# A list scheduler with new costs and due times, and a tail by tiles, in a kernel of sparse attention and mixture of experts

## Chip, cores and metric

The kernel runs on one core of one Trainium2 chip. The metric is the device time of one execution in microseconds (us); of the kernel before three runs were timed, 705.86 to 707.34, median 705.9. The core has a matrix engine (TensorE, PE in the rows; its weight loads stand apart as PEld), a vector engine (VectorE, DVE), a scalar engine (ScalarE, ACT), GpSimd (POOL) and SyncE (SP), which here only issues loads.

## What is computed

Attention over 8 batches, 8 heads, 576 positions and 64 dimensions, whose first four heads look at the last 32 positions and whose other four at every 32nd; then a mixture of 8 experts over the 4608 rows of 512 that result, one expert per row:

```python
scores = q @ k^T / 8
mask = (0 <= rel < 32) for heads 0..3, (rel >= 0) & (pos % 32 equal) for heads 4..7
attn = exp(scores - max) / (sum(exp(scores - max)) + 1e-9)
x = (attn @ v), rows of all heads side by side          # 4608 x 512
logits = x @ w_gate; e = argmax(logits); gate = softmax(logits)[e]
out[row] = gate * (relu(x[row] @ w1[e]) @ w2[e])        # w1 512x1024, w2 1024x512
```

## The kernel before, in words

**Attention.** Only the score blocks that the masks leave are computed. A batch gives five *banks*, each a PSUM tile of 128x512; there are 40 of them, numbered in the order of the batches. A bank's path is `score_ops` (L591 on): PE writes the mask with one matmul (L601, PSUM tag `s`, two buffers) and adds 16 to 32 small products, local ones of 32x64 (L608) or strided ones of 54x54 (L618); DVE takes the maximum (L643) and subtracts it (L648), ACT takes the exponential (L652), DVE sums (L657) and makes the reciprocals of the sums (L659, L660), GpSimd multiplies (L664), PE transposes (L670, tag `t`), and ACT copies that out (L327). Then `product_ops` multiplies with v (L696) into the tags `v` and `w`, one buffer each, and ACT copies the result to `xT`.

**Routing.** Two batches are a *group* (four groups of 1152 rows). Per group `logit_ops` computes the logits (L817, L827), `row_ops` transposes the rows (L874) and writes them with their gate to a table in DRAM, and `route_ops` ranks the rows of each expert (L913) and adds to the lists of row numbers (L960, L964).

**Experts.** A *window* takes up to 4 tiles of 128 rows of one expert: gather from the table (L339), transpose (L421) and split each value into a high and a low part; then in 8 steps the first matmul (L449 to L451, three products per block, tag `t`), relu and split (L456, L459), and the second matmul (L469 to L471) into one accumulator per tile; each finished tile is scaled (L355, L357) and scattered to the output (L347). Weights come in loads of 1 MB, four for a window or slot, and are split by ACT (L330) and DVE (L333, `wlo`). After the second group is routed, windows of two tiles of the experts 0, 2, 4 and 6 (*early windows*) may start while attention goes on; the others follow the last group. Eight *slots* of one tile take the rows over 512 of an expert (L1156 to L1217). A loop that the chip decides on (L1255) would take further slots; with these inputs it turns no times.

**What sets the order.** Every step is an `Op` with an engine, a cost, dependences, a due time (`pri`) and the buffers it takes and gives. `Plan.run` imitates the engines: it picks, for the engine that can start first, the operation with the earliest due time among those that can start within `LOOK`, and emits it. So costs and due times, made from constants as `PACE`, `LEAD` and `FILL0` at the file's head, set the order in which each engine's queue is written, and each engine works its queue in that order. `Plan.issue` (L170 on) holds what the planner believes of PE: half speed after a quiet stretch, a cost for changing the shape of the array, and a pause where the count of instructions passes a multiple of 256.

Of the kernel before, what the change touches and what calls it, by code (L numbers as in the profile page):

```python
# [18 lines left out]
N = B * S  # L19
# [16 lines left out]
RSLOT = 8  # L36
# [6 lines left out]
XTAGS = ("yy", "yy", "vw", "vw")  # L43
# [5 lines left out]
PACE = 5.69  # L49
PACE2 = 4  # L50
LAG = 5.0
LEAD = 48.87
ROWLAG = 2.0
FILL0 = 4.87
FILLW = 40.13
WLEAD = 20.91
WSPL = 3.63
SLOTP = 1987.69
BASEP = 2000.0
GLEAD = 38.84  # L60
TLEAD = 22.28
# [38 lines left out]
FORM_COST = 1.14  # L100
LOOK = 0.3


class Op:
    def __init__(self, eng, cost, fn, deps, pri, take, give, form, nbytes, rate, ins):
        self.eng, self.cost, self.fn, self.pri, self.take, self.give = eng, cost, fn, pri, take, give
        self.form, self.nbytes, self.rate, self.ins = form, nbytes, rate, ins
# [11 lines left out]
class Plan:  # L119


    def __init__(self, bufs):
# [12 lines left out]
        self.hold = True  # L135

# [3 lines left out]
    def add(self, eng, cost, fn, deps=(), pri=0.0, take=(), give=(), form=FULL, nbytes=0, rate=380e3, ins=1):  # L140
        op = Op(eng, cost, fn, deps, pri, list(take), list(give), form, nbytes, rate, ins)
        op.hold = self.hold
        if nbytes and eng != POOL:
            lane = Token("lane", 1)
            op.take.append(lane)
            op.give.append(lane)
# [23 lines left out]
    def issue(self, op, start):  # L170
# [3 lines left out]
        if e == PE:  # L174
# [8 lines left out]
            end = start + op.cost / self.speed(start)  # L183
            done = end + SETTLE[e]
            x = start
            while x < end:
                w = int(x // 3.4133)
                y = min(end, (w + 1) * 3.4133)
                if y <= x:
                    y = end  # L190
                self.busy[w] = self.busy.get(w, 0.0) + y - x
                x = y
        if op.nbytes:
            self.dma = max(end + 0.9, self.dma) + op.nbytes / op.rate
            done = self.dma + 0.9
        self.t[e] = end
# [10 lines left out]
    def run(self, held=False):  # L207
# [5 lines left out]
        for op in ops:  # L213
            for d in op.deps:
# [7 lines left out]
        while must:  # L222
# [26 lines left out]
            for s in op.succ:  # L249
                s.left -= 1  # L250
                if s.left == 0:
                    s.at = max(d.done for d in s.deps)
# [16 lines left out]
def moe_attn(ctx, tc, lqk, vl, sqk, vs, wg, wcat, blob, out):  # L269
# [14 lines left out]
                 "route": 1, "sl": 2, "xge": 4, "xe": 1, "ye": 2, "xgm": 9, "xtm": 2, "yp": 5, "sx": 2, "shr": 2, "shh": 2,  # L284
# [76 lines left out]
    def weights(source, deps, pri, pools, after_row=None):  # L361
# [11 lines left out]
        ld = add(SP, 0.45, load, deps, pri, take=[traw], nbytes=128 * CHW * 4)  # L373
        parts = []
        for h in range(2):
# [8 lines left out]
            def lo(sl=sl):  # L384
                split_lo(w["raw"][:, sl], w["hi"][:, sl], w["lo"][:, sl])

            a = add(ACT, 1.05, hi, [ld] + parts[-1:], pri + WLEAD - WSPL + 0.2 * h, take=[twhl] if h == 0 else (), give=[traw])
            d = add(DVE, 1.23, lo, [a], pri + WLEAD - WSPL + 0.2 * h, give=[traw])
# [3 lines left out]
    def window(e, nt, idc, odc, deps, pri, pace, gp, xp, yp_, names, pools, rows=N + 1, width=512, vtags="vw", ytags=YTAGS):  # L392
# [6 lines left out]
        for t in range(nt):  # L399
# [6 lines left out]
            gs.append(add(POOL, 1.0, g, deps, pri - GLEAD, take=[tk], nbytes=128 * XW * 4, rate=250e3))  # L406
# [3 lines left out]
        for dc in range(4):  # L410
# [18 lines left out]
            p = before = add(PE, 0.109 * nt, tr, gs + [before], pri - TLEAD + 2.5 * dc, take=[tv] + ([txx] if dc == 0 else []), ins=2 * nt)  # L429
# [4 lines left out]
        prev = []  # L434
        last = None
        for c in range(NCH):
            p0 = pri + 2 * c * pace
            w, parts, twhl = weights(lambda e=e, c=c: wcat[(e * NCH + c) * 128:(e * NCH + c + 1) * 128, :], (), p0 - WLEAD, pools)
            for fl in range(2):
# [22 lines left out]
                def mm2(w=w, fl=fl, j=j, b=b):  # L462
# [3 lines left out]
                    for t in range(nt):  # L466
                        ts = slice(t * 128, (t + 1) * 128)
# [904 lines left out]
```

## Time and profile before

| what | us |
|---|---|
| three runs, median (lowest to highest) | 705.9 (705.86 to 707.34) |
| the profiled execution, its own time | 708.59 |
| its span, first to last instruction | 706.8 |
| PE busy (share of the span) | 641.9 (91%) |
| DVE busy | 449.1 (64%) |
| ACT busy | 350.5 (50%) |
| GpSimd busy | 147.0 (21%) |
| mean granted clock of TensorE | 0.958 |

PE's busy time counts matmuls whose ends are modelled, so that a busy PE may still be slow: at half the clock, or with products that follow each other loosely. Idle time of an engine is put down to what ended it; "issue" is idle time that no wait in the profile explains. The span is cut below at three moments: the first expert matmul, the last entry in the lists of rows, and the last matmul.

### The profile page before, as it was taken

The page shows a single profiled execution, that of the slowest core. Times are in us where ns is not written, and L with a number is a line of the kernel's source. Part 1 is how long each engine was busy: PE and PEld are TensorE (multiplying, and loading weights), DVE is VectorE, ACT ScalarE, POOL GpSimd, SP SyncE. Part 2 cuts the span into 40 slices and gives each one's busy share as a digit, 9 for nine tenths or more (in the row PEclk, how much of TensorE's full clock was granted, in tenths as well). Part 3 has the DMA queues.
Part 4 walks back from the last instruction along what each step waited for, and adds up shares of the span by engine and source line. Part 5 has one row for each costly group of instructions (what it writes and reads, how often), then busy time and mean ns, then how long its engine had stood idle before and what let it go on. Part 6 is the DMA issues. An engine that isn't in the chain of part 4 may idle for free.

```text
span 706.8 us, 16724 instructions
## 1 busy us (share of the span) xinstructions
PE 641.9 (91%) x7013; PEld 541.2 (77%) x7020; DVE 449.1 (64%) x791; ACT 350.5 (50%) x601; POOL 147.0 (21%) x189
## 2 busy tenths in 40 slices
PE   5788878799999888999999899999699999999992
PEld 3666666688678677988888798788698888898881
DVE  4576867665786769995555577556467555687210
ACT  2454555456375654464444565545466545576110
POOL 1222321410322424011102303020500300241002
PEclk9698999899999999999999999999899999999996
DMA  9887666835574476576344668565745854692001
GB/s 348 347 317 274 233 220 219 285 118 197 196 260 157 148 263 247 200 274 247 127 184 161 245 233 307 186 255 196 279 161 181 287 189 175 206 348 108 30 1 61
DMA packets 31949, 149.65 MB, mean 212 GB/s; under 512 B 4861, under 2 KB 4861, under 8 KB 21632
## 3 DMA queue, kind: packets, MB, share of 16 engines
q1 hardware_dynamic: 19584, 118.24, 46.1%
q0 software_dynamic: 6432, 20.26, 8.0%
q10 hardware_dynamic: 5856, 10.07, 3.8%
q8 instruction: 56, 0.92, 0.5%
q14 instruction: 21, 0.17, 0.1%
HBM read 129.38 MB, written 20.22 MB: 212 GB/s over the span
## 4 chain that ended last, share of the span: by engine, by line
PE 48%; issue 32%; DVE 7%; POOL 5%; DMA 4%; ACT 2%; POOLq 0%; ACTq 0%; DVEq 0%
PE t L449 4%; PE t L450 3%; PE t L451 3%; PE v L696 3%; PE t L670 3%; PE s L618 3%; POOL out_dram L347 3%; PE s L608 3%; PE y L469 3%; PE y L471 3%; PE y L470 3%; POOL xg L339 2%; DVE wlo L333 2%; PE t L1187 1%; PE t L1188 1%
## 5 line engine op out<-in xcount | busy, mean ns | idle before, releaser
L333 DVE TENSOR_TENSOR wlo<-raw,whi 128x1024 fp32r<-128x1024 f32 x160 | 195.1, 1236 | 57.1 <-ACT whi L330 54.9
L330 ACT CAST whi<-raw 128x1024 fp32r<-128x1024 f32 x160 | 164.6, 1049 | 21.9 <-PE w L1217 10.9
L449 PE MATMUL t<-xh,whi 128*128 128x256 f32 (+1 forms) x384 | 127.2, 331 | 0.0
L451 PE MATMUL t<-xh,wlo 128*128 128x256 f32 (+1 forms) x384 | 122.8, 320 | 0.0
L450 PE MATMUL t<-xl,whi 128*128 128x256 f32 (+1 forms) x384 | 122.5, 319 | 0.2 <-issue 0.2
L456 ACT ACTIVATE hh<-t 128x256 fp32r<-128x256 f32 (+1 forms) x96 | 43.6, 455 | 119.6 <-PE t L451 109.6
L459 DVE SCALAR_TENSOR_TENSOR hl<-t,hh 128x256 fp32r<-128x256 f32 (+1 forms) x96 | 48.5, 508 | 76.8 <-ACT hh L456 75.7
L469 PE MATMUL y<-whi,hh 128*128 128x512 f32 x192 | 79.5, 414 | 2.2 <-ACT hh L456 2.2
L450 PEld LDWEIGHTS t<-xl,whi 128*128 128x128 f32 x384 | 73.2, 191 | 5.9
L451 PEld LDWEIGHTS t<-xh,wlo 128*128 128x128 f32 x384 | 73.1, 190 | 6.0 <-issue 0.3
L449 PEld LDWEIGHTS t<-xh,whi 128*128 128x128 f32 x384 | 73.0, 190 | 6.0
L471 PE MATMUL y<-whi,hl 128*128 128x512 f32 x192 | 76.2, 397 | 0.5 <-DVE hl L459 0.5
L470 PE MATMUL y<-wlo,hh 128*128 128x512 f32 x192 | 75.8, 395 | 0.0
L664 POOL TENSOR_TENSOR prob<-prob,ri 128x512 f32<-128x512 f32 x40 | 43.2, 1082 | 138.3 <-DVE ri L660 72.3
L347 POOL DMA_INDIRECT out_dram<-y,soids x8 | 9.4, 1174 | 208.2 <-DVE y L357 207.9
L643 DVE TENSOR_REDUCE nm<-s 128x8 f32<-128x512 f32 x40 | 27.3, 683 | 32.1 <-PE s L618 17.4
L471 PEld LDWEIGHTS y<-whi,hl 128*128 128x128 f32 x192 | 36.3, 189 | 9.8 <-DVE hl L459 1.5
L469 PEld LDWEIGHTS y<-whi,hh 128*128 128x128 f32 x192 | 36.3, 189 | 7.9 <-ACT hh L456 2.4
L347 POOL DMA_INDIRECT out_dram<-y,oids x24 | 29.9, 1245 | 55.4 <-DVE y L357 44.6
L470 PEld LDWEIGHTS y<-wlo,hh 128*128 128x128 f32 x192 | 36.4, 190 | 5.5
L652 ACT ACTIVATE prob<-prob 128x512 f32<-128x512 f32 x40 | 25.4, 634 | 27.2 <-DVE prob L648 25.7
L327 ACT COPY pT<-t 128x512 f32<-128x512 f32 x40 | 23.1, 590 | 30.7 <-PE t L670 28.9
(166 smaller groups left out, 1253.0 us busy)
## 6 DMA issues: line engine op xcount, KB each, us to landing
raw<-in_wcat_dram SPq DMA_DIRECT2D x80, 1024.0 KB, 5.2
xd<-xr ACTq DMA_DIRECT2D x36, 264.0 KB, 5.2
lqk_sb<-in_lqk_dram SPq DMA_DIRECT2D x16, 592.0 KB, 8.0
sqk_sb<-in_sqk_dram SPq DMA_DIRECT2D x16, 576.0 KB, 6.9
vt<-in_vl_dram SPq DMA_DIRECT2D x16, 576.0 KB, 7.4
vst<-in_vs_dram SPq DMA_DIRECT2D x8, 704.0 KB, 5.3
xg<-xd,ids POOLq DMA_INDIRECT x24
out_dram<-y,oids POOLq DMA_INDIRECT x24
```

The lines of the kernel that those rows point to most:

```text
L330: nc.scalar.copy(out=hi, in_=src)
L333: nc.vector.tensor_tensor(out=lo, in0=src, in1=hi.bitcast(F32), op=ALU.subtract)
L347: i = nc.gpsimd.indirect_dma_start(out=out, out_offset=bass.IndirectOffsetOnAxis(ap=idc, axis=0), in_=y, in_offset=None, bounds_check=N - ...
L449: nc.tensor.matmul(hb[:, 0:n], w["hi"][:, s], xh[:, dc, :], start=(dc == 0), stop=False)
L450: nc.tensor.matmul(hb[:, 0:n], w["hi"][:, s], xl[:, dc, :], start=False, stop=False)
L451: nc.tensor.matmul(hb[:, 0:n], w["lo"][:, s], xh[:, dc, :], start=False, stop=(dc == 3))
L456: nc.scalar.activation(out=b["hh"][:, 0:n], in_=b["hb"][:, 0:n], func=AF.Relu)
L459: nc.vector.scalar_tensor_tensor(out=b["hl"][:, 0:n], in0=b["hb"][:, 0:n], scalar=0.0, in1=b["hh"][:, 0:n].bitcast(F32), op0=ALU.max, op1= ...
L469: nc.tensor.matmul(yb, b["hh"][:, ts], w["hi"][:, s], start=(j == 0), stop=False)
L470: nc.tensor.matmul(yb, b["hh"][:, ts], w["lo"][:, s], start=False, stop=False)
L471: nc.tensor.matmul(yb, b["hl"][:, ts], w["hi"][:, s], start=False, stop=(j == 7))
L664: nc.gpsimd.tensor_tensor(out=pv, in0=pv, in1=st["ri"].unsqueeze(2).broadcast_to([128, 8, 64]), op=ALU.mult)
```

## The change

The planner gets other costs and rules. Its count of PE's instructions starts 63 earlier and takes the local banks at 32 products where it took 16; a new block of 256 may start 2.2 us after it was asked for, plus up to 2.6 us of what the load queue still has to do. Half speed holds from the start of the program, and within an operation. DVE operations that are marked `lock` and those of GpSimd wait for each other. Operations of one `row` name keep their order among themselves. All due-time constants are new.

In the kernel itself: the constants are loaded in two parts (320 of 622 columns first) and the masks made in two steps; the sums go to fixed tiles, and their reciprocals are made by an operation of its own (`inverse`) through three-dimensional views; rows of the first two groups are transposed into `v` and `w` instead of `y`; logits are copied out by ACT instead of DVE; slots gather into a pool of their own; windows of odd experts with an even one before them transpose through `v`, `s`, `s` instead of `v`; the last window does its last two steps of the second matmul tile by tile; and the loop stands in a condition.

```diff
-XTAGS = ("yy", "yy", "vw", "vw")
+XTAGS = ("vw",) * 4
-PACE = 5.69
-PACE2 = 4
-LAG = 5.0
-LEAD = 48.87
-ROWLAG = 2.0
-FILL0 = 4.87
+PACE = 4.44
+PACE2 = 4.84
+LAG = 7.05
+LEAD = 22.82
+ROWLAG = -3.33
+FILL0 = 29.38
...
-            self.half[w] = w > 4 and self.busy.get(w - 1, 0.0) < 0.55 * 3.4133
+            self.half[w] = self.busy.get(w - 1, 0.0) < 0.55 * 3.4133
...
+        if op.eng == DVE and op.lock:
+            r = max(r, self.port[POOL] - 0.13)
+        elif op.eng == POOL:
+            r = max(r, self.port[DVE] - 0.1)
...
-            b = self.count // 256
+            b = (self.count + 63) // 256
             self.count += op.ins
-            if self.count // 256 != b:
-                start = max(start, self.block.get(b - 1, 0.0) + 3.3)
+            while (self.count + 63) // 256 > b:
+                b += 1
+                if b > 1:
+                    asked = self.block.get(b - 1, 0.0)
+                    start = max(start, asked + 2.2 + min(max(self.dma - asked, 0.0), 2.6))
                 self.block[b] = start
...
+                if tail and j >= 6:
+                    steps.append((mm2, d, parts[1], th, twhl))
...
+        if tail:
+            for t in range(nt):
+                for k, (mm2, d, part, th, twhl) in enumerate(steps):
+                    last = add(PE, 3 * 0.229, lambda mm2=mm2, t=t: mm2([t]), [d, part, last], pri + 8.5 * pace + 0.1 * t,
+                               give=[th, twhl], ins=6)
+                ends[t] = last
...
         def c_load():
-            nc.scalar.dma_start(out=cst, in_=blob)
+            nc.scalar.dma_start(out=cst[:, 0:cm], in_=blob[:, 0:cm])
+
+        def c_rest():
+            nc.scalar.dma_start(out=cst[:, cm:], in_=blob[:, cm:])
...
-                sm = small.tile([128, 8], F32, name="sm")
-                nc.vector.tensor_reduce(out=sm, in_=pv, axis=AX.X, op=ALU.add)
-                st["ri"] = small.tile([128, 8], F32, name="ri")
-                nc.vector.tensor_scalar(out=st["ri"], in0=sm, scalar1=1e-9, scalar2=None, op0=ALU.add)
-                nc.vector.reciprocal(out=st["ri"], in_=st["ri"])
+                st["sm"] = sums[sum_turn[0] % 4]
+                sum_turn[0] += 1
+                nc.vector.tensor_reduce(out=st["sm"][:, 0:8], in_=pv, axis=AX.X, op=ALU.add)
+
+            def inverse():
+                sm = st["sm"]
+                se = small.tile([128, 3, 4], F32, name="se", bufs=1)[:, :, 0:3]
+                nc.vector.tensor_scalar(out=se, in0=sm.rearrange("p (a b) -> p a b", a=3), scalar1=1e-9, scalar2=None, op0=ALU.add)
+                st["ri"] = small.tile([128, 9], F32, name="ri")
+                nc.vector.reciprocal(out=st["ri"].rearrange("p (a b) -> p a b", a=3), in_=se)
...
-            nl = {0: 16, 1: 16, 2: 8, 3: 0, 4: 0}[k]
+            nl = {0: 32, 1: 32, 2: 8, 3: 0, 4: 0}[k]
...
-               bpools[:1] if ns else bpools, vtags="v")
+               bpools[:1] if ns else bpools, vtags="vss" if 0 < ENT.get(e - 1, 0) else "v", tail=e == E - 1)
...
-    with tc.For_i(RSLOT, nslots, 1) as s:
+    with tc.If(nslots > RSLOT):
+        with tc.For_i(RSLOT, nslots, 1) as s:
```

Three places show how the order of instructions moves. The first is PE's queue at the program's start, before: a mask (L601), its local products (L608), strided ones (L618), then the first transposes (L670); `s` is the bank, `t` the transposed one.

```order
L601 LDWEIGHTS identb
L601 MATMUL s<-mask_b,identb 128x512
L608 MATMUL s<-lqk_sb 32x64 x8
L618 MATMUL s<-sqk_sb 54x54 x12
L601 LDWEIGHTS identb
L601 MATMUL s<-mask_b,identb 128x512
L670 MATMUL t<-cst,prob 128x128 x4
L696 MATMUL v<-pT,vt 64x32 x2
```

And in the changed kernel from its first row, where L657 is the mask, L664 and L674 the products, L731 the transposes and L758 the product with v:

```order
L657 LDWEIGHTS identb
L657 MATMUL s<-mask_b,identb 128x512
L657 LDWEIGHTS identb
L657 MATMUL s<-mask_b,identb 128x512
L664 MATMUL s<-lqk_sb 32x64 x64
L657 LDWEIGHTS identb
L657 MATMUL s<-mask_b,identb 128x512
L664 MATMUL s<-lqk_sb 32x64 x8
L674 MATMUL s<-sqk_sb 54x54 x12
L657 LDWEIGHTS identb
L657 MATMUL s<-mask_b,identb 128x512
L674 MATMUL s<-sqk_sb 54x54 x8
```

Two masks now stand ahead of two banks' products, and the fourth bank's products ahead of the first bank's transposes, which were behind its mask alone.

The second place is in the second half, where expert 4 begins. Of before, PE's queue: the end of a slot's second matmul (`w`), the transposes of expert 4's two tiles (L421) and of a slot (L1156), all through the one buffer `v`, and the slot's first matmul.

```order
L1215 MATMUL w<-whi,shh 128x512
L1216 MATMUL w<-wlo,shh 128x512
L1217 MATMUL w<-whi,shl 128x512
L421 MATMUL v<-cst,xg 128x128 x2
L1156 MATMUL v<-cst,xg 128x128 x4
L421 MATMUL v<-cst,xg 128x128 x2
L1187 MATMUL t<-whi,sxh 128x256
L1188 MATMUL t<-wlo,sxh 128x256
L1189 MATMUL t<-whi,sxl 128x256
```

DVE's queue of before there: the low parts of weights (`wlo`), and those of the transposed tiles (`xl`, `sxl`), whose end frees `v`.

```order
L333 TENSOR_TENSOR wlo_6806<-raw_6623,whi_6805 128x1024
L333 TENSOR_TENSOR wlo_6813<-raw_6718,whi_6812 128x1024
L333 TENSOR_TENSOR wlo_6806<-raw_6623,whi_6805 128x1024
L333 TENSOR_TENSOR xl_6823<-v_6824,xh_6822 128x256
L333 TENSOR_TENSOR wlo_6813<-raw_6718,whi_6812 128x1024
L333 TENSOR_TENSOR sxl_6838<-v_6839,sxh_6837 128x512
L333 TENSOR_TENSOR xl_6823<-v_6860,xh_6822 128x256
```

PE's queue of the changed kernel at the same work (L449 transposes expert 4's tiles, L1291 to L1293 a slot's second matmul, L497 to L499 that of expert 3's window):

```order
L1274 MATMUL v<-cst,hr 128x128 x2
L497 MATMUL y<-whi,hh 128x512
L498 MATMUL y<-wlo,hh 128x512
L499 MATMUL y<-whi,hl 128x512
L497 MATMUL y<-whi,hh 128x512
L498 MATMUL y<-wlo,hh 128x512
L499 MATMUL y<-whi,hl 128x512
L497 MATMUL s<-whi,hh 128x512
L498 MATMUL s<-wlo,hh 128x512
L499 MATMUL s<-whi,hl 128x512
```

Expert 4's transposes stood together at the window's head, three users of `v` in a row; they are now spread among the matmuls of expert 3's last steps, one pair at a time, with six or more matmuls between two of them.

The third place is the end of PE's queue, before: the last step of the last window, tile by tile (`y`, `y`, `s`, `s`).

```order
L469 MATMUL y<-whi,hh 128x512
L470 MATMUL y<-wlo,hh 128x512
L471 MATMUL y<-whi,hl 128x512
L469 MATMUL s<-whi,hh 128x512
L470 MATMUL s<-wlo,hh 128x512
L471 MATMUL s<-whi,hl 128x512
L469 MATMUL s<-whi,hh 128x512
L470 MATMUL s<-wlo,hh 128x512
L471 MATMUL s<-whi,hl 128x512
```

The same end in the changed kernel, with the numbers of the tiles:

```order
L497 MATMUL s_8407<-whi_8360,hh_8572 128x512
L498 MATMUL s_8407<-wlo_8361,hh_8572 128x512
L499 MATMUL s_8407<-whi_8360,hl_8573 128x512
L497 MATMUL s_8407<-whi_8360,hh_8592 128x512
L498 MATMUL s_8407<-wlo_8361,hh_8592 128x512
L499 MATMUL s_8407<-whi_8360,hl_8593 128x512
L497 MATMUL s_8408<-whi_8360,hh_8572 128x512
L498 MATMUL s_8408<-wlo_8361,hh_8572 128x512
L499 MATMUL s_8408<-whi_8360,hl_8573 128x512
L497 MATMUL s_8408<-whi_8360,hh_8592 128x512
L498 MATMUL s_8408<-wlo_8361,hh_8592 128x512
L499 MATMUL s_8408<-whi_8360,hl_8593 128x512
```

Each tile now gets its last six matmuls together, so that the four tiles are finished six matmuls apart instead of three.

## Rows read from the trace of the kernel before

**Rows 1.** Page: busy time of the engines, and the queue of instruction loads

```profile
PE     641.9 (91%) x7013; PEld 541.2 (77%) x7020; DVE 449.1 (64%) x791; ACT 350.5 (50%) x601; POOL 147.0 (21%) x189
...
q8 instruction: 56, 0.92, 0.5%
```

**Rows 2.** Busy time of four stretches: us, then each engine, granted clock, DMA

```profile
0.00:143.70 143.70, 112.24 (x2884) 87.97 (x2887) 98.15 (x247) 66.22 (x140) 39.45 (x56) 0.88 0.78 280
143.70:255.00 111.30, 106.63 (x1734) 88.08 (x1738) 77.03 (x181) 60.98 (x121) 26.09 (x39) 0.98 0.53 190
255.00:693.00 438.00, 423.03 (x2400) 365.14 (x2398) 273.87 (x364) 222.69 (x342) 78.43 (x89) 0.99 0.55 199
693.00:706.80 13.80, 0.00 (x0) 0.00 (x0) 0.00 (x0) 0.61 (x1) 3.04 (x5) 0.58 0.21 78
```

**Rows 3.** First expert matmul and list entries: count, ns, first to last start

```profile
L449 PE MATMUL t<-xh,whi x384: 274/283/481, 143.7 to 686.6; 128*128 128x256 f32 x128, 128*128 128x512 f32 x64
...
L964 DVE TENSOR_TENSOR idacc<-s,idacc x4: 217/224/225, 83.0 to 255.0; 128x64 f32<-128x64 f32 x4
```

**Rows 4.** Chain that ended last, 0 to 8: start, us, what

```profile
0.76 5.11 DMA cst<-in_blob_dram
...
6.79 0.59 PE s L601
7.38 1.86 PE s L608 x64
```

**Rows 5.** Waits of PE, 0 to 143.7: us in total, times, longest

```profile
PE s L601 <- DVE mask_b L555: 6.8, 1, 6.8
PE v L696 <- issue: 5.3, 4, 3.5
PE s L608 <- issue: 3.9, 3, 2.7
PE t L670 <- POOL prob L664: 2.8, 5, 1.2
PE s L960 <- DVE prob L648: 2.5, 2, 1.5
PE s L618 <- issue: 2.4, 2, 1.9
PE v L696 <- ACT pT L327: 2.2, 4, 0.7
```

**Rows 6.** Timeline: first bank's maximum and transposes, a bank's products, a row's transposes

```profile
9.31 0.69 DVE L643 TENSOR_REDUCE nm<-s 128x8 f32<-128x512 f32 x1 [1.70 <-PE s L608]
...
14.69 0.66 PE L670 MATMUL t<-cst,prob 128*128 128x128 f32 x4 [0.24 <-POOL prob L664]
...
120.00 0.66 PE L874 MATMUL y<-cst,xT 128*128 128x128 f32 x4
120.59 1.10 PE L608 MATMUL s<-lqk_sb 64*32 64x64 f32 x64
```

**Rows 7.** Stretches around 500, columns as in rows 2

```profile
496.40:503.30 6.90, 1.14 (x5) 0.71 (x4) 6.16 (x7) 3.76 (x6) 5.89 (x8) 0.80 0.67 179
503.30:507.40 4.10, 4.09 (x19) 4.09 (x20) 0.42 (x1) 1.13 (x3) 3.19 (x4) 0.50 0.99 394
```

**Rows 8.** Timeline of DVE there

```profile
496.92 3.48 DVE L333 TENSOR_TENSOR wlo<-raw,whi 128x1024 fp32r<-128x1024 f32 x3
```

**Rows 9.** Timeline of the end: last matmul, last scaling, last scatter

```profile
692.50 0.39 PE L471 MATMUL s<-whi,hl 128*128 128x512 f32 x1
...
692.93 0.69 ACT L355 ACTIVATE y<-s,xg 128x512 f32<-128x512 f32 x1 [0.67 <-PE s L471]
...
695.75 0.97 POOL L347 DMA_INDIRECT out_dram<-y,oids  x1 [0.24 <-issue]
```

**Rows 10.** GpSimd's last drain and loop exit: ns min/median/max, first and last start

```profile
L1368 POOLq DRAIN x3: 40/103/6692, 699.3 to 706.6; - x3
...
L1255 POOLq INC_SWDGE_SEM  x1: 1820/1820/1820, 695.8 to 695.8; - x1
```

More of the change, by code (lines that the diff above doesn't have):

```diff
@@ L48 @@
 SLOTS = (0, 1, 1, 2, 1, 2, 1, 0)
-PACE = 5.69
-PACE2 = 4
-LAG = 5.0
-LEAD = 48.87
-ROWLAG = 2.0
-FILL0 = 4.87
+PACE = 4.44
[4 more added lines that the diff above has]
+FILL0 = 29.38
 FILLW = 40.13
-WLEAD = 20.91
-WSPL = 3.63
-SLOTP = 1987.69
+WLEAD = 34.69
+WSPL = 0.03
+SLOTP = 1928.64
 BASEP = 2000.0
-GLEAD = 38.84
-TLEAD = 22.28
+GLEAD = 10.5
+TLEAD = 20.03
+EW = 128 * max(n for _, _, n in PHASES)
+LS_ENG = "ACT"
+POOL_ROUTES = ()
+EARLY_SIDE = ()
 BANK_PAIRS = (
@@ L135, in __init__, with add @@
         self.hold = True
+        self.last = {}
+        self.port = {DVE: 0.0, POOL: 0.0}
     def token(self, pool, users=1):
         return Token(pool, users)
-    def add(self, eng, cost, fn, deps=(), pri=0.0, take=(), give=(), form=FULL, nbytes=0, rate=380e3, ins=1):
-        op = Op(eng, cost, fn, deps, pri, list(take), list(give), form, nbytes, rate, ins)
+    def add(self, eng, cost, fn, deps=(), pri=0.0, take=(), give=(), form=FULL, nbytes=0, rate=380e3, ins=1,
+            row=None, lock=None):
+        op = Op(eng, cost, fn, deps, pri, list(take), list(give), form, nbytes, rate, ins, lock)
         op.hold = self.hold
+        op.behind = self.last.get(row) if row else None
+        if row:
+            self.last[row] = op
         if nbytes and eng != POOL:
@@ L195, in issue @@
             done = self.dma + 0.9
+        if e == DVE and op.lock == "r2":
+            self.port[DVE] = end
+        if e == POOL and op.lock:
+            self.port[POOL] = end
         self.t[e] = end
@@ L213, in run @@
         for op in ops:
-            for d in op.deps:
+            for d in op.deps + ([op.behind] if op.behind else []):
                 if d.done is None:
@@ L359, in moe_attn, with weights @@
     turn = [0]
[L361 removed]
+    def weights(source, deps, pri, pools, side=()):
         w = {}
@@ L371, in load @@
             nc.sync.dma_start(out=w["raw"], in_=source())
-        ld = add(SP, 0.45, load, deps, pri, take=[traw], nbytes=128 * CHW * 4)
+        ld = add(SP, 0.45, load, deps, pri, take=[traw], nbytes=128 * CHW * 4, row=rn)
         parts = []
@@ L488, in sc @@
                 scatter_rows(yv["y"], odc(t))
-            f = add(eng, 0.69 if eng == DVE else 0.62, fin, [last], pri + 8 * pace - 8, take=[tk], give=[ty[t], tg[t]])
+            f = add(eng, 0.69 if eng == DVE else 0.62, fin, [ends[t]], pri + 8 * pace - 8, take=[tk], give=[ty[t], tg[t]])
             add(POOL, 1.1, sc, [f], pri + 8 * pace - 4, give=[tk], nbytes=128 * DM * 4, rate=250e3)
@@ L505, in moe_attn @@
         rt = actx.enter_context(tc.tile_pool(name="rt", bufs=1))
+        sums = [small.tile([128, 9], F32, name=f"sum{k}", bufs=1) for k in range(4)]
+        gsum = small.tile([128, 15], F32, name="gsum", bufs=1)
         loaded = {}
```

274 lines of the change are left out of this document (152 added, 122 removed).

## The prediction

> **What bounds the kernel now.** I read the page's busy times first, then the busy time by stretches, the waits of PE in each stretch, and the timeline where a wait was long. The page says PE 641.9 of 706.8 us, the next engine 64% [rows 1]: the kernel is as long as PE's work plus PE's holes, so the question is where the holes lie. The first expert matmul starts at 143.7 and the last group's entry in the lists of rows is made at 255.0 [rows 3]; the stretches are cut there [rows 2]. In the first, attention alone, PE is busy 112.2 of 143.7 us, at a mean clock of 0.88. In the second, attention mixed with early windows, 106.6 of 111.3. In the third, experts alone, 423.0 of 438. The last 13.8 us have no matmul. The holes are thus 31.5, 4.7, 15.0 and 13.8 us, 65 in all, and the clock costs something on top in the first stretch. No engine but PE is over 68% busy in the first stretch (DVE 98.2 of 143.7): it is not short of an engine, it waits along each bank's path, PE, DVE, ACT, DVE, GpSimd, PE. The changed order holds the same matmuls, so only these holes, and the clock, can give time back.
>
> **The start.** PE's first mask runs at 6.79, and the constants took 5.11 us from their issue [rows 4]. The change loads 320 of 622 columns first. Half of the 5.11 us would be 2.6; but the first products also need queries and keys, which are loaded beside the constants, so the least is 0. I take 1.0 (0 to 2.6), below the middle, because that second load is not made smaller.
>
> **The first stretch.** Its waits fall in two sorts [rows 5]. Three rows end with "issue", where no semaphore held PE: 5.3, 3.9 and 2.4, together 11.6 us. The page counts 56 loads of instructions of 16 KB [rows 1], and the long ones of these waits stand in the small products (L696, L608, L618), which use up a load's worth of instructions fastest. The planner's new rule prices just that. But along the new order the blocks of 256 hold no more PE work than before, and the stretch without experts is longer, so I take a third of it, 4.0 us (0 to 11.6).
> The Trainium skill, page "Runtime: NRT & Kernel Launch", section "Instruction fetch mechanics", says that crossing a 16 KB boundary is mostly hidden, since instructions are issued more slowly than they are fetched. The rows speak against it here, with 11.6 us of PE waiting for nothing that a semaphore explains. By the page this term would be 0 and the sum 4.0 us smaller.
> Three other rows end with data: 2.8 for GpSimd's product, 2.5 and 2.2, together 7.5 us. The first bank's products end at 7.38 + 1.86 = 9.24 [rows 4], its transposes start at 14.69 [rows 6], 5.4 us later; about 0.5 of that is queueing on DVE, so a bank's path takes some 5 us. In the two orders I counted, for each of the first 30 banks, PE's own work between its last product and its transposes, at full-clock durations as the 1.10 us of 64 local products [rows 6], and what it lacks of 5 us. The lack adds up to 19.4 us before and 12.0 in the new order, as its start shows: four banks' products stand ahead of the first transposes. That is 38% less, and 38% of 7.5 us is 2.9 (0 to 7.5).
> The clock: 0.88 over 143.7 us means 143.7 x 0.12 / 0.5 = 34 us at 1.2 instead of 2.4 GHz; with PE busy 78% of them that costs up to 34 x 0.78 / 2 = 13 us. The low stretches follow holes. If a third of the holes go, I expect a quarter of this back: 3 us (0 to 13).
> Against that, the new order starts experts later. Before, 30 of the 40 masks stand ahead of the first expert transposes, afterwards 34. A bank carries 112.2 / 30 = 3.74 us of busy PE. In the first stretch, from 6.8 on, PE is busy 0.82 of the time, so it takes 4.56 us; in the second 0.958, so 3.90. Four banks moved from the second to the first cost 4 x 0.66 = 2.6 us. The bounds are 0 and 4 x 4.56 = 18.2, if the windows that start later fill nothing afterwards.
> Reciprocals: DVE issues the same two instructions a bank, with another view; DVE has a third of the stretch free, so I put 0 (a gain of 0 to 2 us lies inside the bounds above). The logits' copies go to ACT, which is busy 66.2 of 143.7 us: 0. Transposed rows of the first two groups now take `v` and `w`, shared with the products: that is priced as a rival.
>
> **The third stretch.** From 496.4 to 503.3 PE is busy 1.14 of 6.90 us, and the next 4.10 us run at a clock of 0.50 [rows 7]. DVE shows why: three low parts of weights, 3.48 us in one piece from 496.92 [rows 8], stand ahead of the `xl` that frees `v`, and PE's queue holds three users of `v` in a row. In the new order six or more matmuls stand between two users of `v` there, and I found no place after the last list entry where a transpose follows another user of its buffer with under 1.3 us of PE's work between, but for one pair at the very start of that stretch, which before had twice. So 5.76 us of hole go, and half of 4.10 us of slow clock, 2.05: 7.8 us (0 to 12; 0 if such a knot arises at another place, 12 if most of this stretch's 15.0 us goes). The other holes of this stretch, 9 us, I leave as they are: first and second matmuls keep about the same distances.
>
> **The tail.** The last matmul ends at 692.89, the last scaling at 693.62, but the last scatter starts only at 695.75 [rows 9], because four scatters of 1.28 us each queue on GpSimd behind tiles that are ready every 0.69 us. With tiles ready every 1.38 us the queue is gone, and the last scatter starts about 0.28 us after its scaling, at 693.9: 1.85 us earlier. PE pays a little for it: the last relu and its low part need about 1.6 us, and only five matmuls of 0.23 stand in front, so 0.45 us of wait. Net 1.4 us (0.5 to 1.9).
> Behind it GpSimd drains for 6.69 us from 699.3 on [rows 10]. The loop's exit stands ahead of that drain; its INC_SWDGE_SEM ends at 695.75 + 1.82 = 697.57, 1.7 us before the drain starts. With the condition false GpSimd goes from there to its drain. If the drain's length counts from its start, 1.7 us are gained; if it ends by something older, none. I take 1.2, nearer to the row's 1.7.
>
> **Sum.** -1.0 - 4.0 - 2.9 - 3.0 + 2.6 - 7.8 - 1.4 - 1.2 = -18.7 us. The profiled execution took 708.6 and becomes 689.9; the median of the runs without a profile is 2.7 lower, so 705.9 - 18.7 = 687.2. I forecast 687.
>
> **Rivals.**
> *The first stretch gives nothing.* Blocks of instructions are no lighter, and only PE's order moves, not a bank's path. Speaks for it: DVE, ACT and GpSimd have the same work per bank. Against: the counted lack falls by 38%. Then -1.0 + 2.6 - 7.8 - 1.4 - 1.2 = -8.8: 697.
> *The first stretch gives most.* All 11.6 and 7.5 us of its waits go, at the clock as taken: -1.0 - 11.6 - 7.5 - 3.0 + 2.6 - 10.4 = -30.9: 675. For it: one third of the first stretch's time is holes or slow clock. Against: blocks as dense as before.
> *Slower: experts start too late.* The 18 row transposes of the first two groups each hold `v` or `w` for PE's 0.66 us [rows 6] and ACT's copy of about 0.6, 23 us of the buffers that the products with v need, and the first expert matmul moves by four banks' full 18.2 us, without fewer holes before. It decides where that matmul starts later than about 143.7 + 11.4 and the second stretch is no shorter: -1.0 - 10.4 + 18.2 = +6.8: 713. Against: the windows that start later leave the same work for a second stretch that is 96% busy.
> *No change.* The first stretch gives nothing, and a knot like that at 496 comes back at another place: -1.0 + 2.6 - 1.4 - 1.2 = -1.0: 705.
>
> **Chances.** Forecast 0.50, nothing in the first stretch 0.25, most 0.12, slower 0.10, no change 0.03. A change is told from none here beyond 0.2%, 1.4 us. So faster 0.87, within 0.2% 0.03, slower 0.10. The forecast's own range is 679 to 695. The range reaches down to 670, past the second rival, and up to 704, past the first, and leaves out the slower case and a part of the fourth.
>
> **What would show it.** Start: the first mask before 6.3. First stretch: the "issue" rows of PE below 8 us in sum, waits on GpSimd's product below 2, a clock over 0.90, and the first expert matmul at 150 to 156 with the last list entry near 247. Third stretch: no hole of over 3 us at expert 4's transposes and no slow clock behind it. Tail: the last scatter starts about 1.0 us after the last matmul's end instead of 2.9, and the drain starts 1.2 to 1.7 us closer to the last scatter. The forecast is wrong if the last list entry comes at 255 or later, if a hole of 4 us or more arises in the third stretch, or if the drain stays where it was against the last scatter.

## The result, and the profile after

The changed kernel takes 682.1 us (median of 4 runs, 678.7 to 683.6) against 705.9 (702.2 to 707.3) for the kernel before beside it: a ratio of 0.966, interval 0.963 to 0.970. The forecast was 687.0, its own range 679 to 695. The profiled execution of the changed kernel is the lowest of its four (678.7; span 676.9), that of before lies 2.7 us above its median. So the two traces are 29.9 us apart, the medians 23.8. What follows accounts for the 29.9; about 6 of them belong to the choice of executions.

Busy times of the changed kernel, from the page. PE has the work that it had before [rows 1]: 7020 weight loads in both traces (of before, seven records of matmuls are missing). The logits' copies went from VectorE to ScalarE:

```profile
PE 632.8 (93%) x7020; PEld 534.6 (79%) x7020; DVE 428.8 (63%) x784; ACT 356.5 (53%) x613; POOL 145.4 (21%) x185
```

Busy time by stretches, cut at the same three events as [rows 2]: first expert matmul, last list entry, last matmul's end. Columns: stretch, length, PE, PEld, DVE, ACT, POOL, granted clock, DMA share, GB/s.

```profile
0.00:142.20 142.20, 117.38 (x3246) 91.57 (x3246) 97.11 (x269) 76.77 (x160) 42.35 (x62) 0.93 0.79 295
142.20:236.90 94.70, 94.70 (x1396) 80.54 (x1395) 63.60 (x154) 58.21 (x118) 20.96 (x34) 1.00 0.55 190
236.90:665.90 429.00, 420.71 (x2383) 362.46 (x2381) 268.06 (x363) 220.88 (x336) 80.38 (x87) 0.99 0.57 208
665.90:676.90 11.00, 0.01 (x1) 0.00 (x0) 0.00 (x0) 0.69 (x1) 1.74 (x3) 0.65 0.18 67
```

The first two of them, as [rows 3] shows them for before (count, ns, first to last start):

```profile
L477 PE MATMUL t<-xh,whi x384: 276/283/562, 142.2 to 659.0; 128*128 128x256 f32 x128, 128*128 128x512 f32 x64
```

```profile
L1034 DVE TENSOR_TENSOR idacc<-s,idacc x4: 215/216/225, 78.0 to 236.9; 128x64 f32<-128x64 f32 x4
```

A hole here is a stretch's length less PE's busy time. The ledger, from these rows and [rows 2]:

| us | before | after | difference | in the forecast |
|---|---|---|---|---|
| holes up to the last list entry (255.0; 236.9) | 36.1 | 24.8 | -11.3 | -5.3 (start, instructions, data, experts later) |
| holes from there to the last matmul's end | 14.9 | 8.3 | -6.6 | -5.8 |
| behind the last matmul (692.9; 665.9) | 13.9 | 11.0 | -2.9 | -2.6 |
| PE's own busy time, the same matmuls | 641.9 | 632.8 | -9.1 | -5.0 (the clock's two terms) |
| sum | 706.8 | 676.9 | -29.9 | -18.7 |

The last difference is for the most part the clock. In the first two stretches of before 143.7 x 0.12 / 0.5 + 111.3 x 0.02 / 0.5 = 39 us ran at 1.2 GHz, afterwards 142.2 x 0.07 / 0.5 = 20. These 19 us, with PE busy 0.83 of them, are worth 8 by this estimate. What the rest of the 9.1 is, no run shows.

PE's waits in the first stretch of the changed kernel, 0 to 142.2 (us in total, times, longest), answering [rows 5]:

```profile
PE s L657 <- DVE mask_b L607: 6.4, 1, 6.4
PE s L674 <- issue: 5.0, 6, 1.7
PE t L731 <- POOL prob L725: 4.1, 5, 1.3
PE w L758 <- issue: 2.7, 2, 2.1
PE v L758 <- issue: 1.5, 1, 1.5
...
PE s L664 <- issue: 1.0, 2, 0.9
PE v L449 <- issue: 0.7, 1, 0.7
...
PE s L891 <- issue: 0.4, 1, 0.4
```

Before, two more rows of the sort "issue" stand below the three that the prediction added up:

```profile
PE w L696 <- issue: 0.9, 2, 0.4
...
PE s L601 <- issue: 0.5, 1, 0.5
```

All rows of this sort together were 13.0 us and are 11.3; the longest wait fell from 3.5 to 2.1. That most of them are waits for instructions, the traces' records of the 16 KB loads bear out: before, the five waits of 0.7 us and more (9.9 us) end 1.2 to 1.5 us after such a load has landed, and of the seven shorter ones one does; afterwards all twelve in the timeline (10.7 us) end 1.2 to 1.6 us after one. With 22 loads in the stretch before and 25 afterwards, that is 0.45 and 0.43 us a load. Waits for GpSimd's product went up, 2.8 to 4.1. What fell is the rest: all holes of this stretch but the start and the "issue" rows were 31.5 - 6.8 - 13.0 = 11.7 us before, and are 24.8 - 6.4 - 11.3 = 7.1 now, though four more banks lie in it.

PE's waits from 237 to 666, the same view:

```profile
PE v L449 <- DVE xl L354: 5.0, 2, 3.3
PE v L1232 <- DMA xg<-xd,sids: 2.4, 1, 2.4
PE t L479 <- DVE wlo L354: 0.6, 1, 0.6
```

Of before, from 255 to 693, three rows beside those of the knot at 496:

```profile
PE v L421 <- issue: 2.7, 1, 2.7
PE v L1198 <- ACT hr L1193: 2.3, 1, 2.3
PE y L469 <- ACT hh L456: 2.2, 1, 2.2
```

The knot at 496 [rows 7, 8] is gone; a smaller one, which stood at 272 before, has grown and lies at 252, at the transposes of the fourth early window. The timeline of VectorE shows it (start, us, engine, line, operation): 22 instructions for the table of spare rows in one piece, and the low part that PE waits for behind them.

```profile
249.42 0.16 DVE L1133 TENSOR_SCALAR raw<-cnt 128x8 f32<-128x8 f32 x1
...
254.59 0.18 DVE L1163 CAST srow<-raw 128x40 int32<-128x40 f32 x1
254.69 0.42 DVE L354 TENSOR_TENSOR xl<-v,xh 128x256 fp32r<-128x256 f32 x1
```

PE in the same timeline, with the two waits in brackets, and the clock behind them:

```profile
251.44 0.40 PE L499 MATMUL y<-whi,hl 128*128 128x512 f32 x1
255.16 0.44 PE L449 MATMUL v<-cst,xg 128*128 128x128 f32 x2 [3.33 <-DVE xl L354]
...
257.62 0.69 PE L449 MATMUL v<-cst,xg 128*128 128x128 f32 x2 [1.69 <-DVE xl L354]
```

```profile
256.17:263.00 6.83, 5.38 (x25) 5.38 (x26) 6.83 (x9) 2.81 (x5) 1.72 (x1) 0.50 0.35 116
```

The kernel before has the same piece at the same window, with the same `xl` behind it, and PE's 2.7 us stand there. Its profile puts them down to "issue"; in e6 below, which has the same order there, to `xl` (2.6).

```profile
273.97 0.18 DVE L1087 CAST srow<-raw 128x40 int32<-128x40 f32 x1
274.07 0.42 DVE L333 TENSOR_TENSOR xl<-v,xh 128x256 fp32r<-128x256 f32 x1
```

```profile
274.54 0.44 PE L421 MATMUL v<-cst,xg 128*128 128x128 f32 x2 [2.66 <-issue]
```

The end, answering [rows 9, 10]: last matmul, last scaling, last scatter in the timeline, and GpSimd's drain (ns min/median/max, first and last start).

```profile
665.52 0.39 PE L499 MATMUL s<-whi,hl 128*128 128x512 f32 x1
...
665.95 0.69 ACT L376 ACTIVATE y<-s,xg 128x512 f32<-128x512 f32 x1 [2.03 <-PE s L499]
...
666.91 0.97 POOL L368 DMA_INDIRECT out_dram<-y,oids  x1 [0.24 <-ACTq L1331]
```

```profile
L1445 POOLq DRAIN  x3: 40/107/6690, 669.4 to 676.6; - x3
```

The drain of 6690 ns starts at 669.35. The last scatter starts 1.0 us behind the last matmul's end instead of 2.86; from its start to the end of the span it is 10.0 us instead of 11.1, and the drain is as long as before, 6.69.

### The profile page after: what moved, and what is told of

Read it like the earlier page. It is cut to its first block, busy times and chain, and to the rows that moved or that the text cites. A ratio compares the mean times of both kernels' runs of the same rounds, so it can differ in the third digit from the quotient of the medians.

```text
span 676.9 us, 16715 instructions
## 1 busy us (share of the span) xinstructions
PE 632.8 (93%) x7020; PEld 534.6 (79%) x7020; DVE 428.8 (63%) x784; ACT 356.5 (53%) x613; POOL 145.4 (21%) x185
## 4 chain that ended last, share of the span: by engine, by line
PE 58%; issue 25%; DVE 7%; POOL 5%; DMA 3%; ACT 1%; POOLq 0%; DVEq 0%; ACTq 0%
PE t L477 6%; PE t L479 6%; PE t L478 5%; PE y L497 4%; PE y L498 4%; PE y L499 4%; PE v L758 4%; PE t L731 3%; PE s L674 2%; PE s L664 2%; POOL out_dram L368 2%; POOL xg L360 2%; PE s L878 1%; DMA xg<-xd,sids 1%; PE w L1291 1%
## 5 line engine op out<-in xcount | busy, mean ns | idle before, releaser
L351 ACT CAST whi<-raw 128x1024 fp32r<-128x1024 f32 x160 | 166.8, 1049 | 51.7 <-PE w L1293 23.4
L497 PE MATMUL y<-whi,hh 128*128 128x512 f32 x192 | 79.9, 416 | 0.0
L499 PE MATMUL y<-whi,hl 128*128 128x512 f32 x192 | 75.9, 395 | 0.0
L499 PEld LDWEIGHTS y<-whi,hl 128*128 128x128 f32 x192 | 36.3, 189 | 9.1 <-DVE hl L487 0.7
L497 PEld LDWEIGHTS y<-whi,hh 128*128 128x128 f32 x192 | 36.4, 190 | 5.6 <-ACT hh L484 0.4
L1263 PE MATMUL t<-whi,sxh 128*128 128x256 f32 x128 | 36.2, 283 | 0.0
```

The costliest lines, as they stand in the source:

```text
L351: nc.scalar.copy(out=hi, in_=src)
L497: nc.tensor.matmul(yb, b["hh"][:, k], w["hi"][:, s], start=(j == 0), stop=False)
L499: nc.tensor.matmul(yb, b["hl"][:, k], w["hi"][:, s], start=False, stop=(j == 7))
```

## The experiments

They ran in three sets of four, on more than one chip of the same kind, and the kernel before took 714.8, 711.9 and 704.3 us in them (705.9 beside the first result). So only ratios to the kernel before of the same set are compared. Theory A: the planner's two rules (instruction blocks; VectorE and GpSimd waiting for each other) carry the gain up to the lists, the due times the rest. Theory B: the due times alone. Theory C: the attention's edits. Theory D, added later: any redraw of the order falls back.

The holes in this table are worked out as in the ledger, from one profiled execution each, and two executions of one program differ in them: e0 is the changed kernel itself. Only the ratios carry a verdict; the holes show where to look.

| kernel | ratio, 95% interval | last list entry | holes to it | holes behind it | PE busy |
|---|---|---|---|---|---|
| before | 1 | 255.0 | 36.1 | 14.9 | 641.9 |
| changed | 0.966 (0.963-0.970) | 236.9 | 24.8 | 8.3 | 632.8 |
| e0 changed, again | 0.970 (0.966-0.974) | 245.0 | 29.0 | 8.9 | 637.0 |
| e1 old due times | 0.990 (0.985-0.995) | 267.1 | 45.1 | 8.9 | 643.4 |
| e2 new due times only | 1.014 (1.006-1.022) | 249.7 | 39.5 | 28.2 | 644.4 |
| e3 old block rule | 0.979 (0.974-0.985) | 257.6 | 35.2 | 7.8 | 642.1 |
| e4 no wait rule | 0.984 (0.978-0.989) | 245.6 | 26.7 | 14.1 | 640.3 |
| e9 neither rule | 0.990 (0.985-0.994) | 243.7 | 30.3 | 11.6 | 638.1 |
| e5 old attention | 0.976 (0.972-0.981) | 249.2 | 31.0 | 8.5 | 635.8 |
| e5r the same, order kept | 0.971 (0.968-0.974) | 247.9 | 29.9 | 7.0 | 638.1 |
| e8 one due time -1% | 0.968 (0.965-0.971) | 250.9 | 31.0 | 9.2 | 640.5 |
| e6 tail and condition only | 0.998 (0.995-1.000) | 256.7 | 39.7 | 12.1 | 640.2 |
| e7 table in five pieces | 0.956 (0.953-0.959) | 246.4 | 33.6 | 4.0 | 629.8 |
| e7n the same, order redrawn | 0.952 (0.947-0.957) | 235.7 | 25.9 | 2.9 | 626.6 |

**e1 and e2, the due times.** The constants as edited in e1, several to a line here, one to a line in the kernel (e2 is the reverse, in the kernel before):

```diff
-PACE, PACE2, LAG, LEAD, ROWLAG, FILL0 = 4.44, 4.84, 7.05, 22.82, -3.33, 29.38
+PACE, PACE2, LAG, LEAD, ROWLAG, FILL0 = 5.69, 4, 5.0, 48.87, 2.0, 4.87
-WLEAD, WSPL, SLOTP, GLEAD, TLEAD = 34.69, 0.03, 1928.64, 10.5, 20.03
+WLEAD, WSPL, SLOTP, GLEAD, TLEAD = 20.91, 3.63, 1987.69, 38.84, 22.28
-FORM_COST, LOOK = 0.71, 0.05
+FORM_COST, LOOK = 1.14, 0.3
```

> The changed kernel with all the old due times, the old price of a change of matmul form (1.14) and the old look-ahead (0.3); the planner's two new rules and the edits in the attention stay. Theory A (the two rules, instruction blocks and the waiting of VectorE and GpSimd for each other, carry the gain up to the expert lists, the due times the gain behind them): the last list entry comes near 240 us, within 4 us of the changed kernel's 236.9, a hole of some us is back in the third stretch, and the time is 686 to 694. Theory B (the due times carry nearly all): the last list entry comes at 250 or later and the time is 698 to 706. Theory C (the edits in the attention carry it): as A in the front, 684 to 692.

> The kernel before with the new due times, form price and look-ahead alone; nothing else of the change. Theory A: the front stays near the old one, last list entry at 248 to 256 us, and the time is 696 to 706, or above it since the new due times were not made for the old rules. Theory B: the last list entry falls to 236 to 242 and the time to 682 to 690. Theory C: as A.

e1 keeps only a third of the gain, as B said, and loses it in the front, where A had seen none of the due times' work: PE waits 13.9 us for GpSimd's product. But e2 is slower than the kernel before, so B falls too. PE's longest sums of waits in e1 and in e2:

```profile
PE t L731 <- POOL prob L725: 13.9, 13, 6.5
```

```profile
PE v L421 <- DMA xg<-xd,ids: 10.9, 6, 3.4
PE t L670 <- POOL prob L664: 7.8, 7, 1.9
```

The new due times ask for an expert's rows 10.5 us ahead instead of 38.84. On the old planner six gathers come too late for it (10.9 us); in the changed kernel the wait for an expert's rows is 0.2 in sum. Neither the new due times alone nor the rest without them has the gain.

**e3, e4 and e9, the planner's rules.** e3 undoes the first edit, e4 the second, e9 both.

```diff
-            b = (self.count + 63) // 256
+            b = self.count // 256
...
-            while (self.count + 63) // 256 > b:
-                b += 1
-                if b > 1:
-                    asked = self.block.get(b - 1, 0.0)
-                    start = max(start, asked + 2.2 + min(max(self.dma - asked, 0.0), 2.6))
+            if self.count // 256 != b:
+                start = max(start, self.block.get(b - 1, 0.0) + 3.3)
...
-            nl = {0: 32, 1: 32, 2: 8, 3: 0, 4: 0}[k]
+            nl = {0: 16, 1: 16, 2: 8, 3: 0, 4: 0}[k]
```

```diff
-        if op.eng == DVE and op.lock:
-            r = max(r, self.port[POOL] - 0.13)
-        elif op.eng == POOL:
-            r = max(r, self.port[DVE] - 0.1)
```

> The changed kernel with the old rule for TensorE's instruction blocks (a boundary each 256 counted, 3.3 us behind the boundary before, no look at the transfers) and the old count of instructions in a bank; the rule on VectorE and GpSimd, the due times and the attention's edits stay. Theory A: the longest waits for instructions on TensorE come back to 3 us and more in the first stretch, the last list entry falls back by 5 to 10 us (242 to 247) and the time is 686 to 693. Theories B and C: within 3 us of the changed kernel, 679 to 685.

> The changed kernel without the planner's rule that VectorE and GpSimd wait for each other; the rule on instruction blocks, the due times and the attention's edits stay. The changed kernel is at 0.970 of the kernel before on the chip of the last four runs, and 0.979 without the rule on instruction blocks. If both rules carry the order, this one loses about as much: 0.975 to 0.982, with TensorE's waits on GpSimd's product up by 2 us or more in the first stretch. If the rule on instruction blocks alone carries it: 0.966 to 0.973.

> The changed kernel with neither of the planner's new rules: the old planner with the new due times and the attention's edits. The same due times on the old planner with the old attention gave 1.014. If the new due times only fit a planner that knows the blocks and the waits, this is near that run: 0.995 to 1.014. If the rules add what the last two runs say one by one (0.9 % for the blocks, as much at most for the waits): 0.979 to 0.990. If it is the attention's edits that make the due times fit: 0.970 to 0.979.

The block rule is worth 0.9% (0.979 against 0.970 for e0; the intervals just miss each other), in the front: 6 us more holes and 5 us more busy time than e0, the last list entry at 257.6, single waits of 3.0 and 2.3 us. Of these 6 us only 1.8 stand in "issue" rows (15.2 us up to the last list entry, 13.4 in e0), and e9, without the rule as well, has 10.3. So how the rule earns its part is open; that it does so by shorter waits for instructions is not shown. PE's waits in e3 up to 148 us:

```profile
PE t L728 <- POOL prob L722: 6.3, 6, 2.3
PE s L661 <- issue: 4.6, 2, 2.3
PE w L755 <- issue: 3.5, 2, 3.0
```

The rule on VectorE and GpSimd is worth 1.4%, but not where I expected it: the front holds fewer holes than e0's, and 5.2 us more lie behind the lists. PE's waits in e4 from 245.6 to 681:

```profile
PE v L445 <- DMA xg<-xd,ids: 5.5, 5, 2.2
PE v L445 <- DVE xl L350: 4.6, 1, 4.6
```

Gathers late again, as in e2: gathers are issued on GpSimd, the engine that this rule times. That the rule brings the planner's GpSimd closer to the chip's, so that 10.5 us of lead suffice, fits e2, e4 and e9 (4.1 us of this wait), but no run shows it by itself. Both rules together are 2.0% (e9), about the sum of the two. The planner's other new parts (half speed from the start and within an operation, the order kept by `row`, other costs) stay in e3, e4 and e9; no run takes them out alone.

**e5 and e5r, the attention's edits.** e5 undoes all of them and lets the planner draw a new order. e5r keeps each of PE's instructions in the changed kernel's place, the rows' transposes on their new buffers too, and writes the reciprocals and the logits' copy the old way:

```diff
                 nc.vector.tensor_reduce(out=st["sm"][:, 0:8], in_=pv, axis=AX.X, op=ALU.add)
...
+                st["ri"] = small.tile([128, 8], F32, name="ri")
+                nc.vector.tensor_scalar(out=st["ri"], in0=sm[:, 0:8], scalar1=1e-9, scalar2=None, op0=ALU.add)
+                nc.vector.reciprocal(out=st["ri"], in_=st["ri"])
...
-                if LS_ENG == ACT:
+                if LS_ENG == DVE:
```

> The changed kernel with the attention's edits undone: the reciprocals again in the same piece as the sums and in front of GpSimd's product, the copy of the logits on VectorE, the rows' transposes on the old buffers; planner and due times stay new. Theory A: GpSimd's products are again late by 2 to 3 us in sum in the first stretch, last list entry 238 to 242, time 682 to 687. Theory B: within 3 us of the changed kernel. Theory C: last list entry at 248 or later, time 692 or more.

> The changed kernel with every instruction of TensorE in the changed kernel's place, but the reciprocals again written right behind their sum (with two plain instructions, in the sum's place on VectorE) and the copy of the logits on VectorE: the attention's edits undone without a new order. Theory A (planner and due times carry the change): within 4 us of the changed kernel, ratio 0.966 to 0.972, since each product starts at most 0.2 to 0.4 us earlier or later. Theory C (the attention's edits carry): waits on GpSimd's product rise by 3 us or more in the first stretch and the ratio is 0.976 or more, as in the run with a new order (0.976).

In place, the edits are worth 0.1%, within both intervals; the wait for GpSimd's product is even shorter. PE's waits on it in e0 and in e5r:

```profile
PE t L731 <- POOL prob L725: 3.7, 5, 1.1
```

```profile
PE t L731 <- POOL prob L725: 3.2, 5, 0.9
```

C falls for the reciprocals and the logits' copies; the buffers of the rows' transposes were changed back in e5 alone. What e5 loses beyond e5r, 0.5%, is not clear of the noise (the intervals overlap); it may come by the order that the planner draws for other pieces, but that is not shown. e2 and e9 (1.014, 0.990) differ by the attention's edits, the constants' load, the tail and the planner's other new parts, and no run tells which of them makes the difference.

**e0 and e8, the draw.** e0 is the changed kernel once more, e8 changes one number in it.

```diff
-PACE = 4.44
+PACE = 4.40
```

> The changed kernel as it is, once more, on the chip of the runs that follow and against the kernel before on that chip, since the chip of the first four experiments ran the kernel before 1.3 % longer than the first chip. If the gain is the order's own it is there on every chip: ratio 0.963 to 0.970. If part of it was the chip's (the first comparison's profiled run was the lowest of its four), the ratio is nearer 0.975.

> The changed kernel with one due time moved by one hundredth: the spacing of expert blocks 4.40 in place of 4.44. No rule and no instruction changes, but the order is drawn anew. If the planner's rules carry the gain whatever the numbers are, the ratio stays within 0.963 to 0.971. If the gain hangs on this one set of due times (theory D: the due times are fitted to this order, and any other draw falls back), holes of 2 to 4 us are back somewhere behind 240 us and the ratio is 0.974 to 0.985, as in the runs without the block rule (0.979) and without the attention's edits (0.976).

The gain repeats (21.7 us, 711.9 to 690.2), and it survives a redraw. D falls for a small step. e1 and e2, with nearly all due times changed, don't keep the gain.

**e6, the end alone.** In the kernel before, the last expert's last two blocks run their second product tile by tile, and the spare rows' loop stands in a condition:

```diff
+        ends = [last] * nt
+        if tail:
+            for t in range(nt):
+                for k, (mm2, d, part, th, twhl) in enumerate(steps):
+                    last = add(PE, 3 * 0.229, lambda mm2=mm2, t=t: mm2([t]), [d, part, last], pri + 8.5 * pace + 0.1 * t,
+                               give=[th, twhl], ins=6)
+                ends[t] = last
...
+    with tc.If(nslots > RSLOT):
```

> The kernel before with two parts of the change alone, both at the end of the program: the last two blocks of the last expert go tile by tile through their second product, so that each tile's scaling and scatter need not wait for the others, and the loop over spare rows stands in a condition. By the prediction's terms 1.4 us from the tail and 1.2 us from the drain and the exit: 2.6 us, ratio 0.996 (0.994 to 0.998); the last scatter starts about 1.0 us behind the last matmul instead of 2.86. If the drain waits for the earlier scatters anyway, only a fraction of a microsecond shows: 0.999 to 1.000.

0.9975 (0.9948 to 1.0002) is 1.8 us, not told from nothing by the time alone. The trace tells more. Last matmul, last scatter and drain of e6:

```profile
691.57 0.39 PE L471 MATMUL s<-whi,hl 128*128 128x512 f32 x1
```

```profile
692.96 0.97 POOL L347 DMA_INDIRECT out_dram<-y,oids  x1 [0.25 <-ACTq L1267]
```

```profile
L1381 POOLq DRAIN  x3: 40/107/6690, 695.4 to 702.6; - x3
```

From the last matmul's end to the end of the span it is 702.9 - 691.96 = 10.9 us instead of 13.9: 3.0 us, and 2.6 were forecast.

**e7 and e7n, a better version.** The table of spare rows (22 instructions in the trace, not the 27 of the expectation) becomes five pieces in a chain, so that other VectorE work may stand between them; e7n is e7 with e8's number.

```diff
-    o_st = add(DVE, 6.2, slot_tables, [o_ids], SLOTP, take=[traw])
+    o_st = add(DVE, 1.2, table_a, [o_ids], SLOTP, take=[traw])
+    for part, cost in ((table_b, 0.9), (table_c, 1.05), (table_d, 1.05), (table_e, 1.25)):
+        o_st = add(DVE, cost, part, [o_st], SLOTP)
```

> The changed kernel with the table of spare rows (one piece of 27 VectorE instructions, 249.4 to 254.8 us in its trace) cut into five pieces, so that other VectorE work can stand between them. In the changed kernel TensorE waits 3.33 and 1.69 us at 251.8 and 255.9 for xl, which stands behind that piece, and the granted clock is one half from 256.2 to 263.0. If the piece is what costs there, both waits and the half clock go: 5.0 us and some 2.5 to 3.4 us, ratio to the kernel before 0.954 to 0.960, about 1 % under the changed kernel's. If the wait only moves to another tile (the spare list needs the table, and the order behind it is drawn anew), the time is within 3 us of the changed kernel.

> The kernel with the table of spare rows in five pieces (0.956 of the kernel before, against 0.970 of the changed kernel beside it), with the spacing of expert blocks at 4.40 in place of 4.44, so that the order is drawn anew. If the pieces carry the gain, the long wait for xl behind the table stays away and the ratio is 0.953 to 0.960. If the gain was this one draw's luck, the ratio is back at 0.965 to 0.971, as the changed kernel's is with the same nudge (0.968).

680.9 us beside 690.2 for the changed kernel in the same set; the intervals of the ratios don't meet. VectorE in e7: after the first piece (four instructions) both `xl`, a scaling and then a weight's low part go first.

```profile
258.75 0.42 DVE L1142 TENSOR_REDUCE raw<-raw 128x8 f32<-128x256 f32 x1
259.27 0.42 DVE L354 TENSOR_TENSOR xl<-v,xh 128x256 fp32r<-128x256 f32 x1
259.61 0.41 DVE L354 TENSOR_TENSOR xl<-w,xh 128x256 fp32r<-128x256 f32 x1
...
260.60 1.22 DVE L354 TENSOR_TENSOR wlo<-raw,whi 128x1024 fp32r<-128x1024 f32 x1
```

PE's wait for `xl` behind the last list entry, in e0 and in e7:

```profile
PE v L449 <- DVE xl L354: 4.8, 2, 3.5
```

```profile
PE v L449 <- DVE xl L354: 0.3, 1, 0.3
```

Busy time of e0 (first) and e7 (second) from the last list entry to the last matmul:

```profile
245.00:674.90 429.90, 421.05 (x2382) 362.65 (x2380) 267.95 (x363) 221.06 (x337) 80.24 (x87) 0.98 0.57 207
```

```profile
246.40:667.40 421.00, 417.03 (x2382) 358.84 (x2381) 267.24 (x363) 220.08 (x336) 81.26 (x87) 1.00 0.59 209
```

8.9 us in this stretch alone: 4.9 of holes and 4.0 of busy time, with a mean clock of 1.00 instead of 0.98. Redrawn, the gain stays (0.952).

## Why the prediction was right, point by point

The direction and the two largest places held, and the time lies in the forecast's own range. That the sum came so near is luck in part: several terms failed by their own tests, and holes went for which the forecast had no term. Step by step:

- **Start, -1.0.** Right in sign, too large: the first mask runs at 6.42 instead of 6.79, 0.4 us. It was to be before 6.3.
- **Instruction waits, -4.0.** By its own test (below 8 us in sum) this step failed: 11.3 us, where all such rows had 13.0. The waits that end behind a load of instructions cost as much a load as before (0.43 us, 0.45). The rule on blocks is worth 0.9% all the same (e3), but not by this sum. The Trainium skill, page "Runtime: NRT & Kernel Launch", section "Instruction fetch mechanics", calls such crossings mostly hidden. These traces speak against it still: 10.7 us of waits in the first stretch of the changed kernel end 1.2 to 1.6 us after a load of 16 KB has landed.
- **Data waits, -2.9.** Too small: I applied 38% to the 7.5 us of three listed rows, and all such holes fell from 11.7 to 7.1. That this is 39% says nothing for the counted lack: the one row that the lack should shorten, named as the sign, GpSimd's product below 2 us, went the other way (2.8 to 4.1).
- **Clock, -3.0 and -2.05 of the late knot.** Under-sized: PE's busy time fell by 9.1 us. I tied the clock to a quarter of its loss for a third of the holes; low time in the first two stretches halved, 39 to 20 us.
- **Experts later, +2.6.** This step failed. The first expert matmul is at 142.2 (144.6 in e0), not at 150 to 156, although four more banks lie ahead of it. A bank takes 142.2 / 34 = 4.2 us of the first stretch instead of 143.7 / 30 = 4.8. I had priced the move at the old pace and counted the new pace elsewhere. And the second stretch, shorter by four banks, has no hole at all in this execution, where it had 4.7 us; the forecast had no term for these. e0 has 4.0 us there, so this part belongs to the one execution.
- **The knot at 496, -5.8 of holes.** Gone, as said, and no hole of over 3 us is left at expert 4's transposes. I had looked for other knots in PE's queue alone, by the work between two users of a buffer, and not at what VectorE holds in front of the `xl` that frees it. So I left the 2.7 us at the fourth early window's transposes as they were; behind the table's piece they grew to 5.0 (e7 shows that cause by removing it). Of the other late holes, 2.3 and 2.2 us went, and one for the spare rows' gather rose to 2.4; the net was -6.6.
- **Tail and drain, -2.6.** Right: -1.86 from the last matmul to the last scatter and -1.1 from there to the end, a little under the 1.2 of the sign; e6 alone shows 3.0. Of the 0.45 us that PE was to pay, the table of waits shows nothing.

The forecast's sum is 11.2 us short of the trace's. Holes up to the lists make 6.0 of it (2.6 of them the failed step on the experts), the clock 4.1, the rest 1.1. Beside the second comparison (-21.7 us) the same sum is 3 us short. The slower rival's deciding point, experts at 155 or later, did not come; "the first stretch gives nothing" (697) and "most" (675) lie on both sides of the result.

What stays open: how much of the gain is the rules' by their truth and how much by due times chosen to fit them. e1, e2 and e9 show that they have the gain only together (0.990, 1.014 and 0.990 apart, 0.970 together).

## What to carry to other kernels

When a change alters a scheduler's model and its due times together, price them together: here either half alone gave a third of the gain or a loss. Price moved work at the pace of the new order, and do not make the clock's term too small where holes go: here the low time halved where a third of the holes went. Look for knots in the queue of the engine that frees a buffer, not only in that of the engine that waits for it. A long piece of VectorE instructions that a planner can't cut is worth cutting: five pieces for 22 instructions gave 1.4% here.

## What the runs showed of the hardware

- GpSimd's last drain takes 6.69 us in the kernel before (6692 ns), the changed kernel and e6 (6690 ns), wherever it starts. So each microsecond taken from what stands ahead of it is a microsecond of the span: it was 695.75 + 3.57 = 699.32 before, and 666.91 + 2.44 = 669.35 after.
- Waits of PE that no semaphore explains follow the loads of its instructions: in the first stretch of the two traces 17 of them, the five and the twelve named above (0.2 to 3.5 us long), end 1.2 to 1.6 us after a load of 16 KB has landed.
- The same program does not run alike twice. e0's six runs, all on one chip, took 685.7 to 693.9 us, with a mean clock of 0.978 in the fastest and 0.964 in the slowest. The traces of e0 and of the changed kernel, the same program in two sets that may have run on two chips, differ in the same way: the last list entry comes at 245.0 and 236.9, and the clock of 100 to 143.7 us is 0.88 in e0 and 1.00 in the other. The same four transposes take 1.12 us in e0 and 0.66 in the changed kernel, in the timeline of PE:

```profile
131.06 1.12 PE L731 MATMUL t<-cst,prob 128*128 128x128 f32 x4
```

```profile
128.90 0.66 PE L731 MATMUL t<-cst,prob 128*128 128x128 f32 x4
```

So one trace of each kernel does not place a gain to within some 8 us; the ratios over several runs (0.966 and 0.970) agree much better.
